# New load order, a split first load of v, and new rules for joined visits in a fused retention and MLP kernel

## The chip, the cores and the metric

The kernel runs on one core of one Trainium2 chip. A core has TensorE (PE in the profile), VectorE (DVE), ScalarE (ACT), GpSimd (POOL) and SyncE (SP), which work at the same time and wait for each other through semaphores. DMAs are issued from the queues of SP, ACT and POOL. The metric is device time in microseconds for the whole kernel; lower is better.

## The reference

A retention layer (attention without softmax, its scores weighted by a decay that depends on the head) feeds a two-layer MLP with exact GELU. With 8 batches, 8 heads, 576 positions and head size 64 there are 4608 tokens of width 512; the MLP is 512 to 2048 to 512.

```python
scores = scale * np.matmul(q, k.transpose(0, 1, 3, 2))
gamma = 1.0 - 2.0 ** (-5.0 - np.arange(H, dtype=np.float32))
rel = pos[:, None] - pos[None, :]
Dmat = np.where(rel >= 0, gamma[:, None, None] ** rel[None, :, :], 0.0)
attn = np.matmul(scores * Dmat[None], v)
x = attn.transpose(0, 2, 1, 3).reshape(B * S, H * D)
h = x @ w_in
g = 0.5 * h * (1.0 + erf(h * inv_sqrt2))
out = g @ w_out
```

## The kernel before

**Tiling.** The 576 positions of a batch are cut into four chunks of 128 and a tail of 64. A unit is one chunk of one batch (or the tails of two batches), so there are 36 units of 128 tokens; four units make one block of 512 tokens for the MLP, and there are nine blocks. Units 0 to 3 (the first chunk of four batches) are handled one by one. From unit 4 on, units go in groups: a group of two is the same chunk of two batches, a group of one is a pair of tails. There are 22 groups: 0 to 3 are single units, 4 to 9 are the other three chunks of batches 0 to 3, 10 and 11 their tails, 12 to 19 the four chunks of batches 4 to 7, 20 and 21 their tails.

**Retention of a group.** Inside a chunk the scores q k are formed directly; what earlier chunks contribute comes through a running state per head. The steps of a group are: q and k are turned so that the head dimension lies on partitions (on PE for groups 0 to 5, in `turn`, line 518; on DVE for later ones, in `turn_dve`, line 544, with a copy on ACT in `apart`); `scores` (line 576) on PE with the mask on DVE (line 620, or 615 for units 0 to 3); `scaled_v` (line 629), v times a decay per position, on DVE, ACT or POOL; `inner` (line 668), masked scores times v on PE; `state` (line 696), the new state on PE with an addition on DVE; `cross` (line 743), q times the old state on PE; `evacuate` (line 762), which writes the block's activations x as bf16, on DVE (line 788) with a factor per position (`dqT`), or on ACT or DVE for units 0 to 3. Scores, and `inner` with `state` and `cross`, are short runs of small matmuls on parts of the PE array; a run of them between two stretches of MLP matmuls is called a visit here.

**MLP.** The first layer (`mlp1`, or `mlp1_fast` for blocks 6 to 8) and the second layer (`mlp2` for half of block 0, `mlp2_fast` for the rest) are full 128 x 128 matmuls. The fast forms use seven products in place of eight and need sums of weights and activations, made on DVE (`w_out_sums` at line 873, `g_sum` at line 886, `w_in_sums` at line 987, `x_sum` at line 1006). Block 0 starts its first layer by unit and by piece of w_in (256 columns), as these come in.

**Loads.** The first q and k of unit 0 come in float32 over SP's and ACT's queues, and v of unit 0 behind q on SP's queue; DVE and ACT cast them to bf16. All else is loaded by POOL, which casts on the way. Its order is written out by hand in `ORDER` (line 379): `wi` and `wo` are pieces of w_in and w_out, `q`, `k`, `v` and a number are loads of a unit (v is loaded for both units of a group at once from unit 4 on), `n` is a second copy of k for the state, `dq` makes one of the `dqT` factors on POOL, and `io` makes constants. `v0`, `n4` and `n6` in that list issue nothing. POOL's DMAs use eight semaphores in turn, so the ninth load waits until the first has landed. Loads of groups after 12 follow from `reload` when their buffers come free.

**The planner.** The program is written out by a simulation in the kernel's own Python code. It keeps a clock per engine (`T`), an estimated landing time per load (`land`, from `sw_dma`), and emits instructions in the order in which they become ready by these estimates. What it emits is then fixed: each engine runs its instructions in that order and waits at each for its real inputs. In each round (line 1304) `fire` issues loads, casts and side work on DVE and ACT; then PE takes, in this order, a due retention step, else an MLP step, else a retention visit that waited for a partner. While PE would idle early on, `warm` (line 1257) puts in matmuls on zeros.

The rules that bear on the change:

- `s_ready` (line 1285): the next group's scores may run if its units are at most three blocks ahead of the first layer's block (`N_XB` = 4 buffers for x), and if the number of scored units stays at or below `AHEAD + RATE * b1`, where b1 is the number of first-layer blocks done.
- Line 1328: a group is `tied` to its neighbour (same chunk, the other pair of batches) if its number is at least `VISIT` and retention is more than `LEAD` units ahead of the MLP. Then both are visited together, unless nothing else is ready. `NEAR` sets for how long some MLP steps are held back when the joint visit is near.
- `STATE10` is the earliest time for the state of units 2 and 3; `MSK_AT` the earliest time at which DVE makes the mask (`make_msk`, lines 211 to 214); `ARRIVE` the planner's estimate of the delay of POOL's loads.

Of the kernel before, what the change touches and what calls it, by code (L numbers as in the profile page):

```python
# [9 lines left out]
FP32 = mybir.dt.float32  # L10
# [7 lines left out]
def kernel(  # L18
# [14 lines left out]
    nc = tc.nc  # L33
    ctx.enter_context(tc.manual_schedule())

    B, H, S, D = q.shape
# [4 lines left out]
    HP = H // 2  # L41
    C = 128
# [3 lines left out]
    N_BLK = n_tok // TOK  # L46
# [35 lines left out]
    N_VH = 4  # L82
    VH_ACT = [4, 22, 1]
    N_XB = 4
    AHEAD = 8
    RATE = 5.6
    STORE_AT = 62.0
    CROWD = 66.0
    STATE10 = 36.0
    HOT = 8.0  # L90
    FETCH = 5.0
    ARRIVE = 5.6
    WARM_TO = 24.0
    JOIN = 1
    JOIN_SB = 0.0
    VISIT = 4
    LEAD = 3.0
    NEAR = 1.4
    SLACK, SB, PER_G, PER_B, TURN0 = 1.2, 2.0, 8.0, 20.0, 0.0
    FINE = 0.38  # L100
    FPOOL = 0.6
    N_V = 6
    V0_HW = 1
    N_WARM = 10
    MSK_AT = 20.0
    HK = N_DF // 2

    const = ctx.enter_context(tc.tile_pool(name="const", bufs=1))
# [6 lines left out]
    o_pool = ctx.enter_context(tc.tile_pool(name="o", bufs=4))  # L115
# [26 lines left out]


    first = {}
    for nm, src, eng in (("q32", q, nc.sync), ("k32", k, nc.scalar), ("first_v", v, nc.sync))[:2 + V0_HW]:
        t = first[nm] = o_pool.tile([128, H, D], FP32, tag="o_sb", name=nm)
        eng.dma_start(t, src[0, :, 0:C, :].rearrange("h s d -> s h d"))
    zeros = ld_pool.tile([128, 512], BF16, tag="v", bufs=N_V, name="zeros")
    nc.vector.memset(zeros, 0.0)
    lgh = const.tile([128, H, 1], FP32, name="lgh")  # L150
# [70 lines left out]

    later = [(7.3, "act", 1.4, warm_gelu), (MSK_AT, "dve", 0.8, make_msk)]
    T["act"], T["dve"], T["pool"] = 2.6, 2.9, 1.25
# [12 lines left out]
    land = {}  # L236
    loaded = {}
    land_in, land_out = {}, {}

    def sw_dma(issue, move):  # L240
# [3 lines left out]
        T["pool"] += issue  # L244
        sw[0] = max(sw[0] + move, at + ARRIVE + move - 0.9)
        flying.append(sw[0])
# [16 lines left out]
    def all_loaded():  # L263
        return not ORDER and next_load[0] >= N_G

# [38 lines left out]
    def load(what, i):  # L304
        if what == "io":
            constants()
            return
        if what == "v" and i == 0 and V0_HW:
            return
        if what == "wi":  # L310
            nc.gpsimd.dma_start(w_in[:, :, i * 256:(i + 1) * 256],  # L311
                                moe_w_in[:, i * 256:(i + 1) * 256].rearrange("(c p) f -> p c f", p=128))
# [49 lines left out]
        src = {"q": q, "k": k, "v": v}[what]  # L362
# [8 lines left out]

    tiles_of(0)
    land["q", 0], land["k", 0] = 4.85, 5.5
    if V0_HW:
        land["v", 0] = 6.8
    cast_due = {("q", 0): (loaded[0][0][0], first["q32"]), ("k", 0): (loaded[0][0][1], first["k32"])}
    if V0_HW:
        cast_due["v", 0] = (loaded[0][1], first["first_v"])
    ORDER = ("wi7 io wi0 q1 k2 wi1 k1 k3 v0 v1 q2 wo2 q3 wi5 v2 wo0 wi2 wi3 wi6 v3 wo3 wo4 wi4 wo5 wo1 wo6 n4 q4 "
             "wo7 k4 dq2 v4 k5 q5 q6 q8 q7 k6 k7 v8 v6 k8 k9 q10 n8 n6 k10 k11 q9 dq3 q11 k12 dq0 k13 q12 v12 v10 "  # L380
             "dq4 n10 n12 q13").split()

    def next_order():
        item = ORDER.pop(0)
        what = item.rstrip("0123456789")
        load(what, int(item[len(what):] or 0))
# [5 lines left out]
    def reload():  # L392
        if next_load[0] < N_G:
            g = groups[next_load[0]]
            ORDER.extend([f"{what}{i}" for what in "qk" for i in g] + [f"{what}{g[0]}" for what in ("vn" if len(g) > 1 else "v")])
            next_load[0] += 1
# [7 lines left out]
    def free_time(n, pairs=0):  # L404

        got = sorted((max(free_at[banks[k]], free_at[banks[k + 1]]), k) for k in range(0, 8, 2) if not held & {banks[k], banks[k + 1]})
        if len(got) < pairs:
            return 1e9
        used = {banks[k + x] for _, k in got[:pairs] for x in range(2)}
        rest = sorted(free_at[x] for x in banks if x not in held and x not in used)  # L410
        if len(rest) < n:
            return 1e9
        return max([0.0] + [at for at, _ in got[:pairs]] + rest[:n])

    def bank(shape, dtype, name):

        now = T["pe"]
        def rank(x):
            y = banks[banks.index(x) ^ 1]
            return free_at[x] > now, y not in held and free_at[y] <= now, free_at[x]  # L420
        b = min((x for x in banks if x not in held), key=rank)
        held.add(b)
        return b, view(b, shape[1:], dtype)
# [38 lines left out]
    def fetch_at(n):  # L462

        at = place(count[0])[1]
        wait = piece[0] + FETCH - (256 - at) * 0.0075 if at + n >= 256 else 0.0
        return 0.0 if T["pe"] < 20.0 else wait
# [180 lines left out]
    def out_pairs(n):  # L647
        return 2 if n >= 4 else 0
# [87 lines left out]
    def state_at(bp, ci):  # L736
        at = u_ready.get((bp, ci - 1), 1e9) if ci else 0.0
        first = pair_of[bp, ci][0]
        if group_of[first] in BY_DVE:
            at = max([at] + [land.get(("n", i), 1e9) for i in pair_of[bp, ci]])  # L740
        return max([at, free_time(1)] + [st[i].get("V", 1e9) for i in pair_of[bp, ci]])
# [347 lines left out]
    runs1, runs2 = [], []  # L1089
# [23 lines left out]
    n1 = {t: sum(len(r) for u, r in runs1 if u == t) for t in range(N_BLK)}  # L1113
    n2 = {t: sum(len(r) for u, r in runs2 if u == t) for t in range(N_BLK)}

    def left(runs, t):
        return sum(len(r) for u, r in runs if u == t)

    def at_block(runs, n):
        for t in range(N_BLK):  # L1120
            k_ = left(runs, t)
            if k_:
                return t + 1 - k_ / n[t]
        return float(N_BLK)
# [88 lines left out]
    def fire():  # L1213
        now = T["pe"]
        while ORDER and T["pool"] <= now + 1.5:
            next_order()
# [47 lines left out]
    def attend(*ns):  # L1264
        nonlocal nB
        two = out_banks(ns) if ns[0] >= 4 else ()
        for i in [i for n in ns for i in groups[n]]:
            inner(i)
            nB += 1
        while u_due and state_at(*u_due[0]) <= T["pe"] + 0.2 and not (u_due[0] == (1, 0) and T["pe"] <= STATE10):  # L1270
            state(*u_due[0])
# [7 lines left out]
    def ready_for(n):  # L1279

        bp, ci, _ = units[groups[n][0]]
        at = max(max(st[i].get("R", 1e9), land["v", i] if i in raw else st[i].get("V", 1e9)) for i in groups[n])
        return max(at, u_ready.get((bp, ci - 1), 1e9)) if ci else at

    def s_ready(early=0):
        n = group_of[nA]
        g = groups[n]
        if n < nT and n not in [x[0] for x in apart_due] and g[-1] // 4 <= tM1 + N_XB - 1 and nA + len(g) <= AHEAD + early + RATE * b1:
            return sg[n]["T"]
# [9 lines left out]
    for _ in range(N_WARM):  # L1299
        b, t = bank([128, 512], FP32, "warm")  # L1300
# [3 lines left out]
    while True:  # L1304
# [10 lines left out]
        p2s = [r for u, r in runs2 if r]  # L1315
        final = not p1
        b1 = at_block(runs1, n1)
        tM1 = min(int(b1), N_BLK - 1)
        acts = []
# [3 lines left out]
        if nB < nA:  # L1323
# [3 lines left out]
            ready = ready_for(n)  # L1327
            tied = 4 <= n < N_G - 1 and units[g[0]][1] == units[groups[n + 1][0]][1] and n >= VISIT and nB - 4 * b1 > LEAD
            if tied:
                both = 1e9  # L1330
                if nA > groups[n + 1][-1] and one_piece(384 if len(g) > 1 else 192):
                    both = max(ready, ready_for(n + 1))
                    acts.append((max(both, fetch_at(384 if len(g) > 1 else 192), free_time(len(g) > 1 and units[g[0]][1] < NCI - 1, out_pairs(n))), "AA"))
                hold = both <= now + NEAR
                alone = max(ready, free_time(n < 4, out_pairs(n)))
            else:
                acts.append((max(ready, fetch_at(192 if n >= 4 else 0), free_time(n < 4, out_pairs(n))), "A"))
        for key in u_due[:1]:
            if key != (1, 0) or now > STATE10:
                acts.append((state_at(*key), "U"))  # L1340
# [109 lines left out]
```

## Time and profile before

| | |
|---|---|
| median of 3 runs | 291.1 us (290.45 to 292.38) |
| the profiled execution | 290.68 us, of which the span of instructions is 288.8 us |
| granted clock of PE | 1.00 |
| busy in the span | PE 279.9, DVE 228.3, ACT 181.1, POOL 140.8 us |
| DMA | 31.97 MB in 109260 packets, POOL's queue 21.12 MB |

The profile is one execution, taken by the hardware profiler. In it, a row of a timeline gives the start, the duration, the engine, the source line, the operation, what it writes and reads, how often, and in brackets the idle time before it with what ended this. DMAs are named by what they fill. Line 453 is the helper for every matmul and line 457 the one for every transpose on PE, so these rows are told apart by their operands: `x,w_in` is the first layer, `w_out`, `wt`, `ws` and `s` belong to the MLP too, `q_ld,kT` and `qkT` are scores, `ret,vh` and `ret,early` scores times v, `vh,kn_ld`, `vh,k_ld` and `vh,early` the state, `q_ld,u_sb` is q times the state, and `zeros` is filler. The tile `early` holds q, k and v of units 0 to 3. Line 1220 and line 1223 are the casts of unit 0.

### The profile page before, as it was taken

What the parts mean: (1) busy time and instruction counts of PE and PEld (TensorE: products, weight loads), DVE (VectorE), ACT (ScalarE), POOL (GpSimd) and SP (SyncE); (2) the same over time, 40 slices, a digit from 0 to 9 for tenths busy, and PEclk for the clock granted to TensorE, in tenths of its full rate; (3) what the DMA queues carried; (4) which work ended last, traced back from release to release, by engine and by line L of the source; (5) the groups of instructions that cost most, each with busy time, mean ns of one, the idle gap of its engine ahead of it and who ended that gap; (6) DMA issues with size and microseconds to landing.
All of it is one profiled execution on the core that took longest, in us unless ns stands there. A gap on an engine that the chain in (4) does not pass through costs nothing.

```text
span 288.8 us, 9857 instructions
## 1 busy us (share of the span) xinstructions
PE 279.9 (97%) x4211; PEld 210.2 (73%) x4216; DVE 228.3 (79%) x386; ACT 181.1 (63%) x406; POOL 140.8 (49%) x213
## 2 busy tenths in 40 slices
PE   7899999999999999999999999999999999999994
PEld 3468768788764566666666666777888888888883
DVE  6473297499795689678997799869999999999861
ACT  7556544895758868777787779664545453556421
POOL 8865799798849967878677774000000000000000
PEclk9999999999999999999999999999999999999999
DMA  9999999979998999999999996311020202202014
GB/s 158 168 189 195 190 157 160 207 85 140 130 148 64 141 170 140 143 139 186 136 169 155 91 160 51 76 39 39 2 75 0 76 2 74 75 0 75 36 57 128
DMA packets 109260, 31.97 MB, mean 111 GB/s; under 512 B 85920, under 2 KB 104864, under 8 KB 109216
## 3 DMA queue, kind: packets, MB, share of 16 engines
q0 software_dynamic: 100528, 21.12, 83.3%
q1 hardware_dynamic: 7264, 9.51, 10.3%
q10 hardware_dynamic: 1424, 0.72, 0.9%
q8 instruction: 33, 0.54, 0.8%
q14 instruction: 11, 0.09, 0.1%
HBM read 42.99 MB, written 9.44 MB: 182 GB/s over the span
## 4 chain that ended last, share of the span: by engine, by line
PE 92%; DMA 2%; DVE 2%; issue 1%; POOL 1%; ACT 0%; POOLq 0%; DVEq 0%
PE psum L453 91%; DMA early<-in_q_dram 2%; PE psum L457 1%; DVE x L788 1%; POOL w_in L311 1%; DVE qT L551 0%; DVE u_sb L710 0%; ACT u_acc L712 0%; ACT x L490 0%; DVE u_acc L715 0%; DVE qkT L488 0%; DVE o_sb L904 0%; POOL val L185 0%; POOL pos L187 0%; POOLq L185 0%
## 5 line engine op out<-in xcount | busy, mean ns | idle before, releaser
L453 PE MATMUL psum<-x,w_in 128*128 128x256 bf16 (+2 forms) x784 | 118.3, 297 | 1.3 <-issue 0.5
L453 PEld LDWEIGHTS <-w_in 128*128 128x128 bf16 x784 | 68.8, 98 | 29.4 <-issue 2.5
L453 PEld LDWEIGHTS <-g_all 128*128 128x128 bf16 x576 | 55.4, 98 | 13.9
L453 PE MATMUL psum<-w_out,g_all 128*128 128x256 bf16 (+1 forms) x438 | 58.4, 280 | 0.2
L819 ACT ACTIVATE g_all<-psum 128x512 bf16<-128x512 f32 x64 | 37.6, 595 | 19.3 <-PE psum L453 17.9
L347 POOL DMA_DIRECT2D k_ld<-in_k_dram x64 | 35.0, 564 | 23.4 <-DMA kn_ld<-in_k_dram 11.6
L453 PEld LDWEIGHTS <-s 128*128 128x128 bf16 x408 | 39.4, 98 | 7.5
L620 DVE TENSOR_TENSOR ret<-psum,msk 128x1024 bf16<-128x1024 f32 (+1 forms) x32 | 35.6, 1149 | 8.7 <-PE psum L453 7.3
L637 ACT ACTIVATE vh<-v_ld,dv 128x128 bf16<-128x128 bf16 (+1 forms) x144 | 42.3, 383 | 0.0
L1033 ACT ACTIVATE g_all<-t 128x512 bf16<-128x512 f32 x36 | 22.7, 632 | 28.2 <-DVE t L1041 28.2
L347 POOL DMA_DIRECT2D q_ld<-in_q_dram x64 | 35.2, 567 | 1.2 <-DMA k_ld<-in_k_dram 1.1
L490 ACT COPY t<-psum 128x256 f32<-128x256 f32 (+1 forms) x47 | 20.3, 434 | 23.6 <-PE psum L453 23.4
L453 PE MATMUL psum<-wt,s 128*128 128x256 bf16 x272 | 33.8, 273 | 0.0
L904 DVE TENSOR_TENSOR o_sb<-psum,t 128x256 f32<-128x256 f32 x51 | 21.4, 421 | 11.2 <-PE psum L453 5.8
L1041 DVE TENSOR_TENSOR t<-psum,t 128x512 f32<-128x512 f32 x36 | 24.6, 688 | 2.7 <-ACT t L490 1.1
L822 ACT ACTIVATE g_all<-psum 128x512 bf16<-128x512 f32 (+1 forms) x42 | 20.0, 494 | 7.9 <-PE psum L453 7.1
L488 DVE COPY t<-psum 128x512 f32<-128x512 f32 (+1 forms) x40 | 22.1, 563 | 1.1 <-PE psum L453 1.1
L453 PE MATMUL psum<-x,ws 128*128 128x256 bf16 x144 | 19.5, 273 | 0.0
L453 PE MATMUL psum<-wt,g_all 128*128 128x256 bf16 x136 | 17.5, 273 | 0.0
L453 PE MATMUL psum<-w_out,s 128*128 128x256 bf16 x136 | 17.5, 273 | 0.0
L358 POOL DMA_DIRECT2D v_ld<-in_v_dram x14 | 16.4, 1179 | 2.0 <-issue 0.9
L562 ACT COPY q_ld<-qT 128x1024 bf16<-128x1024 bf16 (+1 forms) x16 | 15.0, 936 | 3.8 <-DVE qT L551 3.0
(102 smaller groups left out, 329.6 us busy)
## 6 DMA issues: line engine op xcount, KB each, us to landing
out_dram<-o_sb SPq DMA_DIRECT2D x31, 256.0 KB, 3.7
q_ld<-in_q_dram POOLq DMA_DIRECT2D x56, 64.0 KB, 5.3
k_ld<-in_k_dram POOLq DMA_DIRECT2D x56, 64.0 KB, 4.9
v_ld<-in_v_dram POOLq DMA_DIRECT2D x14, 256.0 KB, 5.3
kn_ld<-in_k_dram POOLq DMA_DIRECT2D x12, 256.0 KB, 6.9
w_in<-in_moe_w_in_dram POOLq DMA_DIRECT2D x8, 256.0 KB, 8.8
w_out<-in_moe_w_out_dram POOLq DMA_DIRECT2D x8, 256.0 KB, 9.5
q_ld<-in_q_dram POOLq DMA_DIRECT2D x16, 32.0 KB, 4.2
```

Of the source, the lines that this page charges most:

```text
L347: nc.gpsimd.dma_start(qk["qk".index(what)][p0:p0 + 32, 0:HP * per].rearrange("p (h x) -> p h x", h=HP), {"q": q, "k": k}[what][2 * bp + jj ...
L358: nc.gpsimd.dma_start(v_ld.rearrange("p j h d -> p (j h) d"), v[2 * bp:2 * bp + 2, :, ci * C:ci * C + C, :].rearrange("b h s d -> s (b h) d"))
L453: nc.tensor.matmul(*a, **k)
L488: nc.vector.tensor_copy(dst, src)
L490: nc.scalar.copy(dst, src)
L620: nc.vector.tensor_tensor(both.rearrange("p (e h) s -> p e h s", e=2), t, by, op=ALU.mult)
L637: nc.scalar.activation(vh[:, 0:m, h], src[:, :, h], AF.Copy, scale=dv[:, h, ci:ci + 1])
L819: nc.scalar.activation(g_all[:, t % 2, :, m0, :], hT.rearrange("p n (a c) -> p (n a) c", a=2), AF.Gelu)
L822: nc.scalar.activation(g_of(t, 2 * lo // TOK)[:, m0:m0 + n, lo_:lo_ + hi - lo], hT, AF.Gelu)
L904: nc.vector.tensor_tensor(dst, src, f[key], op=ALU.add)
L1033: nc.scalar.activation(g_of(t, part)[:, m0:m0 + 2], src, AF.Gelu)
L1041: nc.vector.tensor_tensor(f[key], f["b"][1], f[key], op=ALU.add)
```

## The change

The diff does five things. First, v of unit 0 is loaded in two halves of four heads each, one on SP's queue behind q, one on ACT's queue behind k; the planner's estimate of its landing goes from 6.8 to 6.2 us, and the switch `V0_HW` is gone. Second, `ORDER` is a new list. Third, the constants of the rules change: the scores' limit from 8 + 5.6 b1 to 35 + 0.4 b1, joined visits from group 8 on instead of 4 and from a lead of -3 units instead of 3, `NEAR` from 1.4 to 3.2 us. Fourth, `STATE10` goes from 36 to 28 us, `ARRIVE` from 5.6 to 5.4, and `MSK_AT` from 20 to -58 us, so that the mask is made as soon as the planner's DVE is free. Fifth, `left` and `at_block` count the steps left per block from a table; they give the same numbers as before. No computation is left out and none is added; the sizes of all loads but the first v are as they were.

```diff
--- before.py
+++ after.py
@@ -82,27 +82,26 @@
     N_VH = 4
     VH_ACT = [4, 22, 1]
     N_XB = 4
-    AHEAD = 8
-    RATE = 5.6
+    AHEAD = 35
+    RATE = 0.4
     STORE_AT = 62.0
     CROWD = 66.0
-    STATE10 = 36.0
+    STATE10 = 28.0
     HOT = 8.0
     FETCH = 5.0
-    ARRIVE = 5.6
+    ARRIVE = 5.4
     WARM_TO = 24.0
     JOIN = 1
     JOIN_SB = 0.0
-    VISIT = 4
-    LEAD = 3.0
-    NEAR = 1.4
+    VISIT = 8
+    LEAD = -3.0
+    NEAR = 3.2
     SLACK, SB, PER_G, PER_B, TURN0 = 1.2, 2.0, 8.0, 20.0, 0.0
     FINE = 0.38
     FPOOL = 0.6
     N_V = 6
-    V0_HW = 1
     N_WARM = 10
-    MSK_AT = 20.0
+    MSK_AT = -58.0
     HK = N_DF // 2
 
     const = ctx.enter_context(tc.tile_pool(name="const", bufs=1))
@@ -142,9 +141,11 @@
 
 
     first = {}
-    for nm, src, eng in (("q32", q, nc.sync), ("k32", k, nc.scalar), ("first_v", v, nc.sync))[:2 + V0_HW]:
-        t = first[nm] = o_pool.tile([128, H, D], FP32, tag="o_sb", name=nm)
-        eng.dma_start(t, src[0, :, 0:C, :].rearrange("h s d -> s h d"))
+    for nm in ("q32", "k32", "first_v"):
+        first[nm] = o_pool.tile([128, H, D], FP32, tag="o_sb", name=nm)
+    for nm, src, eng, h0, h1 in (("q32", q, nc.sync, 0, H), ("k32", k, nc.scalar, 0, H),
+                                 ("first_v", v, nc.sync, 0, HP), ("first_v", v, nc.scalar, HP, H)):
+        eng.dma_start(first[nm][:, h0:h1], src[0, h0:h1, 0:C, :].rearrange("h s d -> s h d"))
     zeros = ld_pool.tile([128, 512], BF16, tag="v", bufs=N_V, name="zeros")
     nc.vector.memset(zeros, 0.0)
     lgh = const.tile([128, H, 1], FP32, name="lgh")
@@ -305,8 +306,6 @@
         if what == "io":
             constants()
             return
-        if what == "v" and i == 0 and V0_HW:
-            return
         if what == "wi":
             nc.gpsimd.dma_start(w_in[:, :, i * 256:(i + 1) * 256],
                                 moe_w_in[:, i * 256:(i + 1) * 256].rearrange("(c p) f -> p c f", p=128))
@@ -371,14 +370,12 @@
 
     tiles_of(0)
     land["q", 0], land["k", 0] = 4.85, 5.5
-    if V0_HW:
-        land["v", 0] = 6.8
+    land["v", 0] = 6.2
     cast_due = {("q", 0): (loaded[0][0][0], first["q32"]), ("k", 0): (loaded[0][0][1], first["k32"])}
-    if V0_HW:
-        cast_due["v", 0] = (loaded[0][1], first["first_v"])
-    ORDER = ("wi7 io wi0 q1 k2 wi1 k1 k3 v0 v1 q2 wo2 q3 wi5 v2 wo0 wi2 wi3 wi6 v3 wo3 wo4 wi4 wo5 wo1 wo6 n4 q4 "
-             "wo7 k4 dq2 v4 k5 q5 q6 q8 q7 k6 k7 v8 v6 k8 k9 q10 n8 n6 k10 k11 q9 dq3 q11 k12 dq0 k13 q12 v12 v10 "
-             "dq4 n10 n12 q13").split()
+    cast_due["v", 0] = (loaded[0][1], first["first_v"])
+    ORDER = ("wi4 io wo2 q2 q1 k1 k2 wi5 wi3 n4 v1 wi1 v2 wi0 wi2 k3 q3 v3 wi7 dq2 wi6 wo6 q4 wo4 q5 wo0 wo1 wo3 "
+             "wo5 k5 wo7 q6 k4 k7 v4 q7 k6 q8 v6 q12 dq0 q9 v12 k9 k13 q10 n8 k11 k8 v8 dq3 k10 q11 v10 k12 n10 "
+             "dq4 q13 n6 n12").split()
 
     def next_order():
         item = ORDER.pop(0)
@@ -1113,12 +1110,14 @@
     n1 = {t: sum(len(r) for u, r in runs1 if u == t) for t in range(N_BLK)}
     n2 = {t: sum(len(r) for u, r in runs2 if u == t) for t in range(N_BLK)}
 
+    of_block = {1: [[r for u, r in runs1 if u == t] for t in range(N_BLK)], 2: [[r for u, r in runs2 if u == t] for t in range(N_BLK)]}
+
     def left(runs, t):
-        return sum(len(r) for u, r in runs if u == t)
+        return sum(map(len, of_block[1 if runs is runs1 else 2][t]))
 
     def at_block(runs, n):
-        for t in range(N_BLK):
-            k_ = left(runs, t)
+        for t, block in enumerate(of_block[1 if runs is runs1 else 2]):
+            k_ = sum(map(len, block))
             if k_:
                 return t + 1 - k_ / n[t]
         return float(N_BLK)
```

## The prediction

> **What bounds the kernel now.** I read the page first, then the busy time by stretches, then PE's timeline where the stretches show loss, then the chain of waits.
>
> ```profile
> span 288.8 us, 9857 instructions
> ```
>
> ```profile
> 0.00:20.00 20.00, 16.60 (x200) 9.11 (x204) 11.82 (x42) 12.06 (x24) 16.05 (x26) 1.00 1.56 170
> 20.00:30.00 10.00, 9.95 (x152) 8.24 (x152) 3.94 (x8) 6.17 (x15) 6.30 (x9) 1.00 1.46 196
> 30.00:40.00 10.00, 9.89 (x112) 6.41 (x112) 5.62 (x10) 3.92 (x9) 8.88 (x13) 1.00 1.89 173
> 40.00:50.00 10.00, 9.99 (x214) 8.33 (x213) 8.01 (x14) 5.57 (x15) 9.88 (x14) 1.00 1.74 162
> 50.00:60.00 10.00, 9.30 (x193) 7.31 (x192) 5.72 (x8) 9.14 (x24) 7.95 (x13) 1.00 1.36 179
> 60.00:85.00 25.00, 24.13 (x433) 19.74 (x431) 22.38 (x30) 17.30 (x39) 19.60 (x29) 1.00 1.48 135
> ```
>
> ```profile
> 85.00:215.00 130.00, 130.00 (x2283) 88.65 (x2282) 108.92 (x162) 94.24 (x224) 72.13 (x113) 1.00 1.01 110
> ```
>
> After the stretch the columns are its length, then busy PE, PEld, DVE, ACT, POOL, PE's granted clock, DMA share and GB/s. PE is the bound: from 85 us on it has no idle time at a granted clock of 1.00. There only fewer changes between retention and MLP can save anything. All waiting lies before 85 us: 3.4 us of the first 20, 0.7 from 50 to 60, 0.9 from 60 to 85. But busy time flatters the start:
>
> ```profile
> 9.81 0.40 PE L457 MATMUL psum<-ident,early 128*128 128x128 bf16 x4 [0.98 <-DMA early<-in_q_dram]
> ...
> 14.08 1.25 PE L453 MATMUL psum<-zeros 128*128 128x512 bf16 x5
> ...
> 15.89 0.41 PE L453 MATMUL psum<-ret,early 128*32 128x128 bf16 x16
> ...
> 18.47 1.50 PE L453 MATMUL psum<-x,w_in 128*128 128x128 bf16 x24 [0.42 <-ACT x L490]
> ```
>
> The zeros rows are warming fillers: PE has nothing useful. It first waits for unit 1's q, and unit 1's first-layer matmuls come only at 18.47. Then PE is full until it needs block 1:
>
> ```profile
> 42.57 0.89 PE psum L457 x16
> ...
> 49.80 1.23 DVE x L788
> ```
>
> ```profile
> 45.14 0.62 PE L453 MATMUL psum<-q_ld,kT 32*128 32x128 bf16 x32
> ...
> 48.17 0.63 PE L453 MATMUL psum<-ret,vh 128*32 128x128 bf16 x32
> ...
> 51.06 1.03 PE L453 MATMUL psum<-x,w_in 128*128 128x256 bf16 x8 [0.24 <-DVE x L788]
> ...
> 75.37 0.36 PE L453 MATMUL psum<-q_ld,u_sb 32*64 32x128 bf16 x20 [0.69 <-issue]
> ...
> 83.39 1.89 PE L453 MATMUL psum<-x,w_in 128*128 128x512 bf16 x8 [0.17 <-DVE x L788]
> ```
>
> The first two rows are of the chain of waits, the others of PE's timeline. Group 4 (units 4 and 5, the first half of block 1) is turned at 42.57, scored at 45.14, multiplied with v at 48.17; DVE writes x until 51.03 and the first layer of block 1 begins at 51.06 after an idle 0.24. PE has then run dry. So filling holes before 20 us is worth only as much as group 4's x comes earlier; else the gain is handed back at 51.
>
> **The order of loads.** What they carry:
>
> ```profile
> q_ld<-in_q_dram POOLq DMA_DIRECT2D x56, 64.0 KB, 5.3
> ...
> v_ld<-in_v_dram POOLq DMA_DIRECT2D x14, 256.0 KB, 5.3
> ...
> w_in<-in_moe_w_in_dram POOLq DMA_DIRECT2D x8, 256.0 KB, 8.8
> w_out<-in_moe_w_out_dram POOLq DMA_DIRECT2D x8, 256.0 KB, 9.5
> ...
> early<-in_q_dram POOLq DMA_DIRECT2D x3, 128.0 KB, 6.9
> ...
> q<-in_q_dram SPq DMA_DIRECT2D x1, 256.0 KB, 4.0
> ```
>
> ```profile
> 30.76 0.74 POOL L337 DMA_DIRECT2D k_ld<-in_k_dram  x1 [0.54 <-DMA w_in<-in_moe_w_in_dram]
> ```
>
> By the stretches 3.40 MB have moved by 20 us, 5.36 by 30, 7.09 by 40. Check on the old order: until its last piece of w_in it needs 12 weight pieces, 9 unit loads and the three first loads, 4992 KB or 5.11 MB, reached at 20 + 1.71/0.196 = 28.7 us. The row shows the eighth issue after it held until that piece landed, near 30.7. So I add 2 us to each time worked out this way.
>
> *First 20 us.* The old order brings w_in 7, 0 and 1 among its first five loads. The new one has w_in 4 and w_out 2, then q2, q1, k1, k2, then w_in 5 and 3, v1, w_in 1. So k1 is complete after 896 KB instead of 1152, 1.4 us earlier at 0.18 MB/us, and v1 after 1664 instead of 1408 KB, 1.4 us later. PE need not hold the product of unit 0 behind q1 (0.98 idle). Unit 0 then has one piece of w_in instead of three, and its other matmuls run where the fillers of 14.08 stand (1.25). Unit 1's product stood at 15.89 and its matmuls at 18.47, since its copy came late on ACT (0.42 idle for it); with the product 0.5 to 1 us later and the copy straight behind it (the cast of v below, as large, takes 0.62), they start near 17.3, 1.2 us earlier. I take 1.2 to 2.2 us of PE time recovered, the upper end being 0.98 + 1.25. The bad end is 1.0 lost, if the two late pieces (16 of 24 matmuls, 1.50 x 2/3) fall into the full stretch.
>
> *Block 1's start.* Old: q5 is the last load of group 4, at 6784 KB = 6.95 MB, 39.2 us. New: q4, q5 and k5 come early among the weights, k4 at 6656 KB = 6.82 MB, 38.4 us, then k7 and v4 at 7040 KB = 7.21 MB, 40.7 us. With 2 us added, k4 lands at 40.4 and v4 at 42.7.
>
> ```profile
> 42.00 2.45 ACT L637 ACTIVATE vh<-v_ld,dv 128x128 bf16<-128x128 bf16 x8
> ```
>
> ```profile
> 45.81 2.36 DVE L620 TENSOR_TENSOR ret<-psum,msk 128x1024 bf16<-128x1024 f32 x2 [1.01 <-PE psum L453]
> ```
>
> From v: 42.7 + 2.45 = 45.2. From k: turning (half of 0.89), its copy (some 0.7, the nearest row being again the cast of 0.62), scores 0.6, mask 2.36: 40.4 + 4.1 = 44.5. So the product could come near 45.2 instead of 48.17, 3 us earlier. But DVE must also make the sums of w_out, whose last piece comes after 6400 instead of 6144 KB, 1.5 us later, and these push towards the mask; I take 2. Block 1's lead (2) and PE's recovered time (1.2 to 2.2) must come together; for the pair I take 1.8 us. Bounds: 0 if block 1 stays at 51, -3 if all of the lead is used, +1.0 from the paragraph above.
>
> **The rules of joining and running ahead.** The scores' limit goes from 8 + 5.6 per block to 35 + 0.4 per block, so only the four x buffers hold them back. The joined visit now needs group 8 or later, but no lead. Read on two visits of each kind:
>
> ```profile
> 98.18 0.63 PE L453 MATMUL psum<-ret,vh 128*32 128x128 bf16 x32
> ...
> 99.34 1.90 PE L453 MATMUL psum<-x,w_in 128*128 128x512 bf16 x8
> ```
>
> ```profile
> 146.80 1.08 PE L453 MATMUL psum<-ret,vh 128*32 128x128 bf16 x64
> ...
> 149.02 1.05 PE L453 MATMUL psum<-w_out,s 128*128 128x256 bf16 x8
> ```
>
> A single visit takes 99.34 - 98.18 = 1.16 us, a joined one 2.22; with one entry fewer (some 0.1) a join saves 0.2. The pairs 14-15, 16-17, 18-19 and both pairs of tails are joined already; groups 8-9 and 12-13 can be new. Two joins, 0.4 us; bounds 0 and -1.0. Groups 6 to 9 reaching their scores sooner takes the two waits for x (0.24 and 0.17) away: 0.4. The stall of 0.69 named issue hangs on where the instruction stream stands, not on data; it may go or come, plus or minus 0.7, and I count nothing.
>
> **Edits with no cost.** v of unit 0:
>
> ```profile
> 1.25 0.57 SPq L147 DMA_DIRECT2D first_v<-in_v_dram  x1
> ```
>
> ```profile
> 7.57 0.62 ACT L1223 CAST early<-first_v 128x512 bf16<-128x512 f32 x1 [0.66 <-DMA first_v<-in_v_dram]
> ```
>
> ACT's cast is done at 8.19, while PE multiplies unit 0 only at 10.1, behind q1. An earlier v gains nothing there. The second half costs ACT one more issue before its first activations, 0.3 to 0.57 us, hidden by the same 0.98 wait; uncovered it costs at most 0.57. The state of units 2 and 3 may run from 28 instead of 36 us: the same 0.4 us of PE elsewhere. The mask moves to the start:
>
> ```profile
> 21.86 0.70 POOL L326 DMA_DIRECT2D w_out<-in_moe_w_out_dram  x1 [0.44 <-DMA w_out<-in_moe_w_out_dram]
> ...
> 22.21 0.37 DVE L212 TENSOR_SCALAR msk<-val 128x128 f32<-128x128 f32 x1
> ...
> 22.62 0.39 DVE L214 COPY msk<-msk 64x64 f32<-64x64 f32 x2
> ```
>
> Its 0.76 us fit the holes that DVE has before its first products, and POOL's issue beside it took 0.70, so I count nothing. The Trainium skill says in "SBUF — State Buffer" (the box on the "DVE blocks DMA" trap) that copies and scalar operations of DVE can lock POOL out of writing descriptors; by it the loads queued behind the mask would slip by up to 0.76 us. The row does not agree.
>
> **Sum.** -1.8 -0.4 -0.4 = -2.6 us. The profiled execution took 290.68 (span 288.8, 1.9 around it), the median of the three runs is 291.1. So 288.1 for such an execution, 288.5 for the median.
>
> **The rivals.** *Deeper gain*: block 1 starts the full 3 us earlier, the 0.69 stall falls away, joins save 0.9: with 0.4 of x waits 5.0 us, 286.1. For it: k4 no longer waits to be turned with a q that comes last. Against: DVE's sums of w_out lie in their way.
>
> *Given back*: group 4's x comes no earlier, since v4 now comes after 7040 KB, before after 6528 KB (6.68 MB, 37.6 + 2 = 39.6 us against 42.7), and the sums come in between; PE runs dry near 50. Only a join or two stays: 290.7.
>
> *Slower, DVE becomes the bound*: with the limit gone one more pair enters before 85 us.
>
> ```profile
> 80.58 1.11 DVE L551 STREAM_TRANSPOSE qT<-q_ld 128x512 f32<-128x512 f32 x1
> 81.52 0.69 DVE L715 TENSOR_TENSOR u_acc<-psum,u_acc 128x512 f32<-128x512 f32 x1
> ...
> 83.25 1.12 DVE L551 STREAM_TRANSPOSE kT<-k_ld 128x512 f32<-128x512 f32 x1
> ```
>
> A pair costs DVE 1.11 + 1.12 + 2.36 + 0.69 + 1.23 = 6.5 us, and from 60 to 85 it has 2.6 free. It decides from 2.6 us of added work on; one whole pair means 3.9 us in which MLP's evacuations are late and PE stands: 291.1 + 3.9 = 295.0. Against it: 4.3 us are free from 50 to 60 (10 - 5.72), and 4.4 from 30 to 40, where the work of such a pair could go if its loads are there.
>
> *The mask blocks POOL*: every load behind the mask's 0.76 us lands that much later and block 1 with them, so 288.5 + 0.8 = 289.3. Against it stands POOL's 0.70 beside the mask. The page "SBUF — State Buffer" of the Trainium skill is the one that would expect it.
>
> **How the numbers follow.** A measurement here tells about 1% from no change: under 288.2 is faster, over 294.0 slower. Forecast 0.46 (287 to 290.2; 0.20 of it faster), deeper gain 0.21 (faster), given back 0.15 (same), DVE 0.15 (all but 0.01 slower), mask 0.03 (same). Faster 0.41, same 0.45, slower 0.14. The range takes in the deeper gain with its bounds (285.2) and ends at 293.0, where the slower case begins to be left out: 0.03 below, 0.14 above.
>
> **What would show it.** Right: no wait for q1 near 9.8; unit 1's matmuls before 17.2; block 1's first layer at 48 to 49.5; two more visits whose products with v are x64; 130 of 130 us busy still in the later part. Wrong: fillers after 20 us, x L788 again ahead of an idle PE near 50, DVE over 24 of 25 us from 60 to 85 with PE waiting, or w_out the releaser of PE between 30 and 40, which would mean that putting w_out 0, 1 and 3 so late was the dear part.

## The result, and the profile after

The changed kernel takes **287.59 us** (median of four runs, 287.03 to 288.46) against 290.94 us for the kernel before, a ratio of 0.988 with an interval of 0.984 to 0.992. So it is faster by about 3.4 us, and 0.9 us below the forecast of 288.5. The profiled execution took 288.46 us with a span of 286.7 (before 290.68 and 288.8): 2.1 us of the gain are in the two traces that can be laid side by side. It is the slowest of the changed kernel's four, so the rest of the gain is in no trace here. Each ratio below is to the kernel before as it was timed alongside (290.8 to 291.2 us), and medians and ratios below leave out the executions that fell into a slower state.

The same stretches as before, changed kernel (length, then busy PE, PEld, DVE, ACT, POOL, granted clock, DMA share, GB/s):

```profile
0.00:20.00 20.00, 16.57 (x208) 9.38 (x208) 14.28 (x47) 11.53 (x24) 17.05 (x26) 1.00 1.50 172
20.00:30.00 10.00, 9.87 (x179) 8.85 (x180) 4.02 (x7) 5.28 (x13) 6.89 (x10) 1.00 1.78 182
30.00:40.00 10.00, 9.99 (x89) 6.13 (x87) 6.71 (x11) 3.12 (x10) 8.50 (x12) 1.00 1.57 174
40.00:50.00 10.00, 8.87 (x202) 7.26 (x200) 7.10 (x11) 5.40 (x14) 8.96 (x13) 1.00 1.72 174
50.00:60.00 10.00, 10.00 (x205) 8.54 (x203) 6.40 (x7) 8.43 (x19) 8.27 (x13) 1.00 1.49 173
60.00:85.00 25.00, 25.00 (x464) 20.02 (x462) 22.13 (x29) 19.80 (x51) 20.98 (x33) 1.00 1.54 141
85.00:215.00 130.00, 129.62 (x2263) 89.48 (x2261) 109.21 (x164) 91.63 (x217) 70.35 (x110) 1.00 1.00 109
```

PE's idle time has moved: 1.13 us in 40 to 50 that were not there before, and none from 50 to 85, where before had 0.70 and 0.87. Added up over these rows, PE idles 5.1 us in both kernels. Busy time hides the gain, since fillers are busy too: 24 now, 29 before.

What tells more is how far PE has come. I count each matmul of the computation at the spacing that matmuls of its size have at full clock (216 ns for 512 columns), fillers as nothing, and ask how much earlier the changed kernel has as much work left as the one before had at a given time:

| at (us, kernel before) | 20 | 40 | 52 | 60 | 74 | 77 | 90 | 215 | end |
|---|---|---|---|---|---|---|---|---|---|
| lead of the changed kernel (us) | 0.8 | 1.0 | 0.1 | 0.9 | 1.0 | 1.9 | 2.2 | 2.1 | 2.1 |

Five matmul records, worth 0.5 us, are missing in the trace of before. By the count of weight loads they lie before 40 us, so only the column of 20 can be too low. The lead is won at the start, lost at 45, won again between 52 and 60, jumps by 0.9 at 75, and stays from 90 on. PE's timeline of the changed kernel, and of DVE the mask product of group 4:

```profile
9.07 0.23 PE L450 MATMUL psum<-ret,early 128*32 128x128 bf16 x2
9.67 0.40 PE L450 MATMUL psum<-ret,early 128*32 128x128 bf16 x14 [0.36 <-DVE ret L612]
10.56 0.40 PE L454 MATMUL psum<-ident,early 128*128 128x128 bf16 x4 [0.49 <-DMA early<-in_q_dram]
...
16.70 1.48 PE L450 MATMUL psum<-x,w_in 128*128 128x128 bf16 x16
...
43.25 0.62 PE L450 MATMUL psum<-q_ld,kT 32*128 32x128 bf16 x32
...
45.94 0.61 PE L454 MATMUL psum<-ident,q_ld 128*128 128x128 bf16 x8 [1.08 <-DMA q_ld<-in_q_dram]
...
48.01 0.63 PE L450 MATMUL psum<-ret,vh 128*32 128x128 bf16 x32
...
51.59 2.69 PE L450 MATMUL psum<-x,w_in 128*128 128x256 bf16 x23
...
93.85 1.08 PE L450 MATMUL psum<-ret,vh 128*32 128x128 bf16 x64
...
118.44 1.08 PE L450 MATMUL psum<-ret,vh 128*32 128x128 bf16 x64
...
123.09 1.03 PE L450 MATMUL psum<-wt,s 128*128 128x256 bf16 x8 [0.33 <-ACT t L487]
```

```profile
43.92 2.35 DVE L617 TENSOR_TENSOR ret<-psum,msk 128x1024 bf16<-128x1024 f32 x2 [0.96 <-PE psum L450]
```

The product of unit 0 no longer stands behind q1, and unit 1's first layer comes at 16.70 instead of 18.47. Group 4 is scored at 43.25 instead of 45.14, and DVE has masked its scores by 46.27, 1.9 us earlier than before (45.81 + 2.36). But its product stands at 48.01, where it stood (48.17), and block 1's first layer begins at 51.59, even after the 51.06 of before. PE's program has the turning of group 5 ahead of that product, and there PE stands 1.08 us for a q. The chain of waits names the load, and SyncE's timeline what goes out at the same time:

```profile
28.94 7.12 DMA w_out<-in_moe_w_out_dram
...
39.69 6.11 DMA q_ld<-in_q_dram
45.80 0.14 issue
45.94 0.61 PE psum L454 x8
```

```profile
40.47 0.84 SPq L1253 DMA_DIRECT2D out_dram<-o_sb  x2
```

This q belongs to unit 7. It is issued at 39.69 and lands after 6.11 us, against a median of 5.5 for such loads in this kernel (5.3 before), while the first two stores of block 0 leave.

The other part of the gain is in rows of the kernel *before*. Its timeline between 52 and 61:

```profile
54.37 2.36 PE L453 MATMUL psum<-x,w_in 128*128 128x256 bf16 x20 [0.30 <-issue]
...
59.47 1.70 PE L453 MATMUL psum<-x,w_in 128*128 128x256 bf16 x14 [0.16 <-issue]
```

With the 0.69 at 75.37 these are three holes in which PE waits for no data. From start to start of the matmuls around them they cost 0.46, 0.33 and 0.90 us, 1.7 together, and the table's lead grows at just these times. The changed kernel has none there. The page's row for PE's instruction queue, the same in both kernels, says what they are:

```profile
q8 instruction: 33, 0.54, 0.8%
```

PE has 4216 matmuls and as many weight loads on the changed kernel's page, so 33 packets of 16 KB carry 256 instructions each: the program comes in pieces, by the same DMA engines as the loads. Counted along the program, each of the three holes stands at the first instruction of a new piece. The trace's records of single packets show that the piece's packet moved 2.6 to 3.5 us after PE had entered the piece ahead, took 0.9 us, and PE went on 1.4 to 1.6 us after its end. Where PE would get through a piece in less than the sum, here 5.1 to 5.8 us, it stands still. The changed kernel is as fast through three pieces of this stretch (entered at 48.5, 53.7 and 67.8, done in 5.2, 4.8 and 5.5 us) and does not stop: there the packets moved 0.7 to 1.6 us after PE had entered the piece ahead. The 256-instruction blocks are what the Trainium skill's page "Runtime: NRT & Kernel Launch" (section "Instruction fetch mechanics") describes; it calls the cost mostly hidden, and the runs below differ.

### The profile page after: what moved, and what is told of

Same layout as the page of the kernel before. It is cut to its first block, busy times and chain, and to the rows that moved or that the text cites. A ratio compares the mean times of both kernels' runs of the same rounds, so it can differ in the third digit from the quotient of the medians.

```text
span 286.7 us, 9851 instructions
## 1 busy us (share of the span) xinstructions
PE 277.8 (97%) x4216; PEld 210.3 (73%) x4216; DVE 229.7 (80%) x387; ACT 176.7 (62%) x403; POOL 141.0 (49%) x213
## 4 chain that ended last, share of the span: by engine, by line
PE 61%; DMA 22%; POOL 12%; issue 2%; ACT 1%; DVE 0%; POOLq 0%
PE psum L450 60%; DMA kn_ld<-in_k_dram 6%; DMA w_out<-in_moe_w_out_dram 6%; DMA q_ld<-in_q_dram 5%; POOL k_ld L346 3%; POOL q_ld L346 2%; DMA v_ld<-in_v_dram 2%; DMA early<-in_q_dram 2%; POOL v_ld L357 2%; DMA k_ld<-in_k_dram 1%; POOL dqT L320 1%; PE psum L454 1%; POOL kn_ld L352 1%; POOL w_in L310 1%; POOL k_ld L336 1%
## 5 line engine op out<-in xcount | busy, mean ns | idle before, releaser
L816 ACT ACTIVATE g_all<-psum 128x512 bf16<-128x512 f32 x64 | 36.9, 592 | 16.4 <-PE psum L450 14.8
L819 ACT ACTIVATE g_all<-psum 128x256 bf16<-128x256 f32 (+1 forms) x43 | 19.5, 488 | 11.2 <-PE psum L450 10.6
L785 DVE TENSOR_TENSOR x<-psum,dqT 128x1024 bf16<-128x1024 f32 (+1 forms) x14 | 15.5, 1137 | 0.1
```

The source lines that it names most:

```text
L816: nc.scalar.activation(g_all[:, t % 2, :, m0, :], hT.rearrange("p n (a c) -> p (n a) c", a=2), AF.Gelu)
L819: nc.scalar.activation(g_of(t, 2 * lo // TOK)[:, m0:m0 + n, lo_:lo_ + hi - lo], hT, AF.Gelu)
```

## The experiments

The questions: is the gain in the holes between 50 and 90 us (theory A below), in the load order (theory B), in the rules of joining and running ahead (theory C), or only in all edits as one plan, so that one edit put back gives a plan with its own waits (theory D)? "Lead" is that of the table above, always over the first profiled execution of the kernel before.

**The load order alone**, on the kernel before (its `ORDER` replaced by the new one):

> The kernel before with the new order of POOL's loads alone; v whole on SyncE's queue and all rules as before. Theory A (the gain sits in the stretch from 50 to 90 us, where holes of PE on instruction fetches and on x went, and the early gain of the new loads is handed back near 45 us): the first layer of block 1 starts no earlier than 50 us, filler and waits of the first 40 us fall by 1 to 1.5 us, and the whole comes out 289 to 292 us, depending on where the fetches fall. Theory B (the load order is the gain): 287 to 288.5 us. Theory C (the new rules of joining and running ahead are the gain): 290.5 to 291.5 us.

292.02 us, ratio 1.004 [1.002, 1.006], at the upper edge of theory A's range and above the other two. The lead is 0.7 us at 52 and 1.5 at 60, the same step as in the changed kernel, falls to 0.4 at 90, is back at 1.8 at 215 and ends at -0.9. PE's timeline in this kernel:

```profile
72.83 1.03 PE L453 MATMUL psum<-wt,g_all 128*128 128x256 bf16 x8 [0.65 <-ACT t L490]
...
82.56 1.03 PE L453 MATMUL psum<-wt,g_all 128*128 128x256 bf16 x8 [0.46 <-ACT t L490]
...
277.83 2.36 PE L453 MATMUL psum<-wt,s 128*128 128x256 bf16 x20 [0.66 <-DVE s L886]
```

The order buys its part of the front, and the planner, fed other landing times, lays out everything behind it anew: PE waits for MLP evacuations on ACT and, at the end, for sums of activations on DVE.

**The rules put back** in the changed kernel:

```diff
-    AHEAD = 35
-    RATE = 0.4
+    AHEAD = 8
+    RATE = 5.6
-    VISIT = 8
-    LEAD = -3.0
-    NEAR = 3.2
+    VISIT = 4
+    LEAD = 3.0
+    NEAR = 1.4
```

> The changed kernel with the five constants of the old rules (limit of scores 8 + 5.6 per block, joins from group 4 and a lead of 3, holding back for 1.4 us); new loads and split v stay. Theory A: 287 to 290 us, by where the fetches fall. Theory B: 287 to 288 us, nothing lost. Theory C: 290.5 to 291.5 us, nearly all of the gain lost; two visits more than in the changed kernel after 85 us, each 0.2 us.

288.07 us, 0.990 [0.988, 0.992]: the rules are worth some 0.2%, which these intervals don't separate from nothing, and theory C is out. `AHEAD` and `RATE` put back alone give the same program on all five engines as the changed kernel, and so does `NEAR`. So the limit on the scores, the largest change to look at, does not bind here.

**v whole**, on SyncE's queue, in the changed kernel:

```diff
-                                 ("first_v", v, nc.sync, 0, HP), ("first_v", v, nc.scalar, HP, H)):
+                                 ("first_v", v, nc.sync, 0, H)):
```

> The changed kernel with v of the first unit whole on SyncE's queue, all instructions otherwise in the same order. From the traces: v lands at about 7.5 instead of 6.6 us, while ScalarE casts it from 7.0 on; its cast moves by 0.5 us and the mask product of the first unit on VectorE (8.3 to 9.6 us) still ends last before PE's product. All theories: within 0.3 us of the changed kernel, 287.3 to 287.9 us. If the split were part of the gain: 288.5 us or more.

287.77 us, 0.988 [0.986, 0.990], lead at the end 2.6 us. The split does nothing that can be measured.

**The first two stores on ScalarE's queue**, in the changed kernel and in the one before:

```diff
-            queue = nc.scalar if ending and (m if len(rows) > 1 else ts % 2 == 0) else nc.sync
+            queue = nc.scalar if (t == 0 and ts < 2) or ending and (m if len(rows) > 1 else ts % 2 == 0) else nc.sync
```

> The changed kernel with the first two stores (rows of block 0) on ScalarE's queue, where they wait for their place in ScalarE's program (after 55 us), instead of SyncE's, which sends them at 40.5 us. If these stores are what delays q of unit 7 (landing 6.1 us after its issue, PE waits 1.1 us for it at 45 us), that wait is gone, the first layer of block 1 starts about 1 us earlier, and the time is 286.5 to 287 us; the two stores then compete with later loads. If POOL's queue alone is late, the wait stays at 1.0 us or more and the time within 0.3 us of 287.6.

> The kernel before with the first two stores on ScalarE's queue, behind its program, instead of at 41.0 and 41.5 us on SyncE's. In the trace of before the load issued at 40.6 us took 5.1 us to land, those before it 2.9 to 4; PE did not wait for it. If what held the changed kernel at 45 us is a matter of its own plan: 290.5 to 291.5 us here, no gain. If stores in general delay the loads and the instruction fetches up to 60 us: 290 us or less, with the holes at 54.4 and 59.5 us smaller.

Changed kernel: 287.23 us, 0.987 [0.985, 0.989]; kernel before: 291.41, 1.002 [0.9995, 1.005]. PE's waits in the changed kernel without and with the edit (total, times, longest):

```profile
PE psum L454 <- DMA q_ld<-in_q_dram: 1.1, 1, 1.1
PE psum L450 <- DMA w_in<-in_moe_w_in_dram: 0.6, 1, 0.6
PE psum L454 <- DMA early<-in_q_dram: 0.5, 1, 0.5
```

```profile
PE psum L450 <- DVE t L485: 0.9, 1, 0.9
...
PE psum L454 <- DMA q_ld<-in_q_dram: 0.4, 1, 0.4
```

The wait for q falls from 1.1 to 0.4, and the lead at 52 us is 1.0 instead of 0.1. That fits stores that held up unit 7's q, but another run speaks against it. The kernel with v whole runs the same instructions in the same order on PE, DVE, ACT and POOL, and SyncE sends these stores at the same time. Of it, SyncE's timeline and PE's:

```profile
40.51 0.85 SPq L1253 DMA_DIRECT2D out_dram<-o_sb  x2
```

```profile
45.06 0.61 PE L454 MATMUL psum<-ident,q_ld 128*128 128x128 bf16 x8 [0.16 <-DMA k_ld<-in_k_dram]
```

There PE waits 0.16 us, and with the old rules, where the stores leave at 40.65, not at all. So the wait of 1.08 belongs to one execution, and the stores are not shown as its cause. In the kernel with the stores moved, a wait of 0.89 for DVE opens at 129.9, and the end is the same. It is the lowest median of all kernels here, but not separable from the changed kernel's.

**State time back, mask time back**, one at a time in the changed kernel (`STATE10 = 36.0`; `MSK_AT = 20.0`):

> The changed kernel with one constant back: the state of units 2 and 3 from 36 us on, not 28. The work itself is 0.35 us of PE, moved by some 8 us. Theory D (the loads, the three timing constants and the rules are one plan; a constant without a cost of its own changes the order of everything behind it): 289.5 to 294 us, with new waits late in the run, as the old rules with the new loads had them after 215 us. Theory A (holes between 50 and 90 us, else nothing): within 1 us of 287.6. Reading it as the prediction did, at no cost: 287.3 to 287.9 us.

> The changed kernel with the mask made from 20 us on, not at the start. The mask is 0.76 us of VectorE. Theory D: 289 to 291 us, with the waits again late. By direct cost: VectorE's first mask product starts 0.7 us sooner (it waited for the mask until 8.3 us) and the time is 287.3 to 287.9 us. If the mask beside POOL's loads had delayed them, loads land up to 0.7 us sooner here.

297.86 us (300.29 in the profiled execution), 1.025 [1.019, 1.031], and 292.44 us, 1.005 [1.003, 1.007]. I had taken both constants as free. PE's waits with the state's time at 36:

```profile
PE psum L450 <- issue: 5.5, 3, 3.1
PE psum L450 <- DVE x L789: 1.8, 1, 1.8
PE psum L454 <- DMA k_ld<-in_k_dram: 1.4, 1, 1.4
```

3.2 us are waits for data at 45 and 52 us, of this plan's own. But 5.5 us wait for nothing, like the holes of before, and larger. With the mask at 20 the lead is 2.3 at 90 as in the changed kernel, and it is lost in three steps: 1.0 us between 150 and 156, where a wait named issue of 0.48 stands, 1.4 between 204 and 222, and 2.1 between 258 and 270 at waits for DVE of 0.33 and 0.75.

**The same program, moved against its pieces.** In the kernel before, four of the ten 128x512 fillers become 32 of 128x64 with the same columns, so that the program is 56 PE instructions longer at its start; all that follows is in the same order on every engine:

```diff
-    for _ in range(N_WARM):
+    for n_ in range(6):
...
+    for n_ in range(32):
+        b, t = bank([128, 512], FP32, "warm")
+        nc.tensor.matmul(t[:, 0:64], lhsT=zeros[:, :128], rhs=zeros[:, 0:64], start=True, stop=True)
+        release(b, 0.0)
+    count[0] += 2.004 * (N_WARM - 6)
```

> The kernel before with the same plan, but its PE program 56 instructions longer at the start: four of the ten first fillers (1.7 us) are replaced by 32 short ones of 64 columns, at the same time in all. So each place where the program goes from one fetched piece of 256 instructions to the next comes 28 matmuls earlier. If the holes named issue hang on where these places lie: the holes at 54.4, 59.5 and 75.4 us go or move, and new ones come where two places are under 5 us apart, inside the joined visits near 150, 173 and 195 us (by the trace 2.4, 3.0 and 1.9 us apart), each 1.5 to 3.5 us; in all 294 to 299 us. If not: 290.5 to 291.5 us and no new holes.

296.41 us, 1.017 [1.013, 1.021]. The hole at 75 is gone. Those at 54 and 59 come 28 matmuls earlier in the program and are longer (1.20 and 0.87 us), and two are new: 2.65 us from 151 on and 1.02 from 201 on. The one expected near 173 did not come. Its waits, and the stretch behind its longest hole:

```profile
PE psum L453 <- issue: 5.7, 4, 2.7
```

```profile
153.90:157.00 3.10, 3.08 (x10) 1.32 (x10) 0.00 (x0) 0.92 (x2) 3.10 (x6) 0.53 1.60 172
```

The same edit in the changed kernel, and in the changed kernel with the state's time at 36:

> The changed kernel with the same 56 instructions more at the start, order the same. Theory A (that the changed kernel has no hole of this kind between 50 and 90 us is where its pieces happen to begin, not its plan): holes of 0.2 to 3 us open somewhere, 289 to 293. Theory D (the new plan is robust against it because its loads leave the queues free): 287.6 +- 0.8, no issue row in its waits over 0.5 us.

> The changed kernel with the state's time at 36 again (300.29 us, three PE waits of the kind issue, 5.5 us together), its program made 56 TensorE instructions longer at the start: four of the 128x512 fillers before the data arrives become 32 of 128x64 with the same work; every engine's order behind them is the same. Theory A (those holes lie where two pieces of program follow each other closely, so where the pieces begin decides): the holes at 98.8 and 139.9 go or move, the time lands away from 300.3 by over 2 us, 293 to 298 if no new ones open. Theory D (the plan with 36 is itself bad: its waits for DVE and for a load, 3.2 us, and the late tail set the time): 300 +- 1, with the issue holes where they were or replaced by waits for data.

295.60 us, 1.014 [1.007, 1.021], and 303.94 us, 1.046 [1.038, 1.054]. So the changed kernel is no more robust than the one before: the 56 instructions cost it some 8 us. Theory A holds in kind, but both its ranges (289 to 293, 293 to 298) were too low. Of the changed kernel so shifted, the waits, the longest hole in PE's timeline, and the stretches behind a hole of 0.74 us and behind the longest:

```profile
PE psum L450 <- issue: 6.9, 6, 3.4
```

```profile
96.53 0.75 PE L450 MATMUL psum<-q_ld,u_sb 32*64 32x128 bf16 x63
100.70 0.24 PE L450 MATMUL psum<-q_ld,u_sb 32*64 32x128 bf16 x1 [3.42 <-issue]
100.87 3.26 PE L450 MATMUL psum<-x,w_in 128*128 128x512 bf16 x9
```

```profile
57.30:62.00 4.70, 4.70 (x51) 4.17 (x51) 1.42 (x2) 2.80 (x5) 4.70 (x8) 1.00 1.68 155
100.70:104.80 4.10, 4.10 (x13) 1.59 (x14) 2.24 (x4) 1.19 (x2) 4.10 (x8) 0.62 1.79 117
101.70:105.10 3.40, 3.40 (x9) 1.21 (x8) 1.52 (x3) 1.19 (x2) 3.40 (x7) 0.50 2.10 140
```

The hole splits one run of 64 equal matmuls, all with their data there, 63 and 1. And it is paid twice: the granted clock is 0.62 in the 4.1 us behind it (0.50 from 101.70 to 105.10), so nine matmuls of 512 columns take 3.26 us, where full clock needs about 2.

**The load order put back** in the changed kernel, and **the three times alone** in the kernel before (`ARRIVE = 5.4`, `STATE10 = 28.0`, `MSK_AT = -58.0`):

> The changed kernel with the old order of POOL's loads. Theory A (the gain is the order's in the first 40 us and the absence of holes): 1.5 us of front gain gone, 289 to 292, and the wait for q of unit 1 near 10 us back. Theory D (order, state time and mask time are one plan; one alone put back gives a new plan with its own waits): worse than before, 292 to 298, with waits for loads past 20 us that neither kernel has.

> The kernel before with only the three time constants of the change (arrival of the first x 5.4, the state's time 28, the mask at the start) and its own load order and rules. My prediction took these as free: 290.9 +- 0.8. Theory D: a new plan with its own waits, off by 2 us or more to the slow side, 293 to 298. Were they the source of the gain, it would be 288 to 289.

295.70 us, 1.016 [1.012, 1.021], and 291.13 us, 1.002 [0.999, 1.006]. For the first, theory D's time was right: its lead is -1.6 at 52 and -5.6 at the end. Its longest waits behind 40 us, beside 1.5 us of holes, are these; the one for a q is as long as the changed kernel's, the others neither kernel has:

```profile
PE psum L450 <- DVE t L485: 1.1, 2, 0.8
PE psum L454 <- DMA q_ld<-in_q_dram: 1.1, 1, 1.1
PE psum L450 <- ACT g_all L816: 1.0, 1, 1.0
```

For the second D was wrong and the prediction right: on the old order the three times cost nothing that can be told. With the old order put back, 293.6 us of a span of 295.1 are left when its holes are taken off, and no clock is lost: here the plan is worse, not its placement. Order and times belong together. Alone, either is worth +0.2 to +0.4% of time; together, still with the old rules and with v split, -1.0%.

**Laid together.** PE's granted clock in these traces is either 1.00 or 0.50 (other values are means over a stretch). Where it falls it stays at 0.50 for 3.4 us (once for twice that), which costs 1.7. The changed kernel's falls only behind PE's last matmul, where it costs nothing:

```profile
275.00:282.90 7.90, 7.90 (x73) 6.87 (x71) 2.62 (x6) 2.23 (x6) 0.00 (x0) 1.00 0.24 68
...
285.80:286.70 0.90, 0.00 (x0) 0.00 (x0) 0.00 (x0) 0.00 (x0) 0.00 (x0) 0.50 0.00 0
```

From the span of each profiled execution I take PE's waits named issue, and 1.7 us for each such stretch while PE still has matmuls:

| kernel | span | issue | clock | what is left |
|---|---|---|---|---|
| before | 288.8 | 1.5 | 0.0 | 287.3 |
| before, 56 more | 295.1 | 5.7 | 1.7 | 287.7 |
| changed | 286.7 | 0.0 | 0.0 | 286.7 |
| changed, 56 more | 294.6 | 6.9 | 1.7 | 286.0 |
| changed, state 36 | 298.5 | 5.5 | 3.4 | 289.6 |
| changed, state 36, 56 more | 304.9 | 9.4 | 6.8 | 288.7 |

In each of the last two kernels one of the stretches at half clock begins at a wait for data, at 53. The last column moves by 0.4 to 0.9 us with the shift, while the span moves by 6 to 8. So the shift acts through these two columns. The change as a plan is worth about 1 us (287.3 - 286.7 = 0.6, or 287.7 - 286.0 = 1.7), some 0.4%. The larger part of the 2.1 us between the two spans, some 1.5, is where the pieces of the program happen to begin: with 56 instructions more on both sides, 295.60 stands against 296.41, and the intervals of the two (1.007 to 1.021, 1.013 to 1.021) overlap. Only one size of shift was tried.

## Why the prediction was right, and where it was not

The total was right, its terms were not; that it came out near is luck. -1.8, -0.4, -0.4 and 0 were forecast, and in the two traces the first gave -0.1, the last -1.7. Of the signs set for a right reading, unit 1's start and the two visits of x64 came; the wait for q1 stayed at half, block 1 came late, and the later part is 129.62 of 130 us busy.

*Front and block 1's start (-1.8).* The first half held: unit 0's product came before q1 and unit 1's matmuls at 16.70, under the 17.2 set for it. PE still waits 0.49 us for q1, one row later. The lead at 40 us is 1.0, against the 1.2 to 2.2 that were to be recovered. The second half failed. The step "block 1's lead (2) and PE's recovered time must come together" wanted block 1's first layer at 48 to 49.5; it came at 51.59. Group 4 was scored and masked 1.9 us earlier, about the 2 that the working took. But it stopped at the mask: PE's program has the turning of group 5 ahead of the product, and in the profiled execution this waited until 45.94 for the q of unit 7, a load that the working did not follow. That is the rival "given back" in effect, 1.1 us of it, by another load than the v4 it named. The lead at 52 us is 0.1. Where that q came sooner, the lead at 52 is still far from the 1.8 of the forecast: some 0.6 with v whole and with the old rules, 1.0 with the stores moved.

*The issue stalls (0, plus or minus 0.7).* This was the dear error of size. The row of 0.69 was read as one event that "hangs on where the instruction stream stands", which is right, but PE's rows hold five waits of that kind, three of them between 52 and 77, and they cost 1.7 us from start to start. All three went. Six of the later kernels show how wide the bound should have been: they hold 1.5 to 9.4 us of it, and four of them lost clock behind it.

*The waits for x (-0.4).* They are gone (0.24 at 51.06, 0.17 at 83.39); from 77 to 90 the lead grows by 0.3. But the lifted limit on the scores, to which the term was put down, is not why: with the old limit the program is the same, and with all the old rules these waits are gone as well.

*The joins (-0.4).* Both new ones came, 8-9 at 93.85 and 12-13 at 118.44, and from 40 us on there are 11 products with v instead of 13. From 90 to 215 us the lead does not grow (2.2 to 2.1): waits such as the 0.33 at 122.76 take the saving back. With the old rules the time is 0.5 us higher, inside the intervals. The mechanism stands, its worth is not shown.

*Edits at no cost.* For the split v that was right. For the mask beside POOL's issues too, as the changed kernel's timeline shows:

```profile
6.74 1.54 POOL L310 DMA_DIRECT2D w_in<-in_moe_w_in_dram  x2
...
7.11 0.47 DVE L213 TENSOR_SCALAR msk<-val 128x128 f32<-128x128 f32 x1
...
7.62 0.68 DVE L215 COPY msk<-msk 64x64 f32<-64x64 f32 x2
...
8.21 0.95 POOL L368 DMA_DIRECT2D early<-in_v_dram  x1
```

The two issues beside the mask take 0.77 us each, as long as those of the same kind later (0.74 to 0.83). The lockout that the Trainium skill's "SBUF — State Buffer" describes (the box on the "DVE blocks DMA" trap) would have shown here as a gap or a long issue; the next row, 0.95, begins when the mask is nearly done. As an argument about plans the step failed: "the same 0.4 us of PE elsewhere" held for the state's time on the old order (1.002). On the new one the same constant makes the profiled span 11.8 us longer, with 5.5 us of holes, 3.4 of lost clock and 3.2 of waits for data in it; 2.9 are left when holes and clock are taken off (289.6 against 286.7), or 4.6 if the stretch at half clock that its own waits brought at 53 is counted with the plan.

*The rivals.* DVE did not become the bound, and the lifted limit, from which that rival starts, changes nothing: 22.13 of 25 us from 60 to 85, with PE full, less than the 22.38 before. The deeper gain had the right entry for the stall and the wrong one for block 1; the time fell between it and the forecast.

What stays open: why the packet of a piece moves 0.7 us after PE has entered the piece ahead in one place and 3.5 in another. That it shares the engines with the loads is in the page's rows; a kernel with the loads thinned out around a hole was not tried. Why unit 7's q came late in one execution is not known. What costs the kernels with one edit put back their lead after 90 us was read from their waits and not tried singly.

## What to carry to other kernels

In a kernel whose order is planned from landing times, an edit to one constant is an edit to everything behind it: cost the plan, and test edits in the company they will have. Before a gain of 1% is put down to a change in such a kernel, move its program by some dozens of instructions on both sides; as far as the gain goes, it was placement. A wait named issue on a full engine belongs in the range with its possible size, not with the size of the one that the trace happens to show.

## What the hardware showed

Instruction fetch can stop a full PE for 0.2 to 4.0 us, in the middle of a run of equal matmuls with their data in place. A program of 33 pieces had no such wait over 0.1 us in the changed kernel and 9.4 us of them in the worst one.

The granted clock falls behind the longer holes, to 0.50 for 3.4 us (the row from 101.70 above). Over the 3 to 4 us behind a hole the mean is 0.53 behind 2.65 us, 0.64 behind 3.07, 0.62 behind 3.42. In the kernel with the state's time at 36 and 56 instructions more it is 0.52 over the 6 us behind 3.96, two such stretches in a row:

```profile
167.00:173.00 6.00, 5.97 (x23) 3.01 (x23) 4.38 (x5) 2.00 (x4) 4.03 (x7) 0.52 0.82 67
```

Behind 0.74 us (the stretch from 57.30 above) it stays at 1.00, and behind 1.80 us too. But in the kernel with the three times alone a wait for data of 1.31 us, with PE little busy just before, is followed by 4 us at 0.61, and with the state's time at 36 one of 1.78 us by a stretch at 0.50. So the length alone does not decide. A rule of the Trainium skill, in "TensorE: Matmul & The Clock Gate" ("Why this matters for your kernels"), is to leave no gap of more than about 3 us; the runs agree above 3 us, and show the clock lost behind shorter ones as well.
